# A new order of the ACT, DVE, POOL and SP queues in a fused attention, mixture and channel-mixing kernel on one Trainium2 core

## The chip, the cores and the metric

The kernel runs on one core of one Trainium2 chip. Its time is the device time of that core in microseconds. Three runs of the kernel before took 461.11, 462.46 and 463.20 us, so the median is 462.46 us. Every trace is one profiled execution. The engines are named as in the profile: PE is TensorE, PEld is its weight load, DVE is VectorE, ACT is ScalarE, POOL is GpSimd, and SP only issues DMAs here.

## The reference, cut to what matters

All data are float32. The batch is 2 and the sequence has 768 tokens.

```python
# A: attention with 8 heads of 64; a window of 96 keys behind the query and 8 global keys, a slope per head
scores = q @ k.T / 8 - slope[h] * dist          # masked outside window and global keys
x = softmax(scores) @ v                         # heads joined to 512 columns
# D: top 2 of 4 experts, each a causal attention with one head of 64
w = softmax over the two largest of x @ w_gate
x = sum over e in top2: w[e] * (softmax(causal((x @ wq[e]) @ (x @ wk[e]).T / 8)) @ (x @ wv[e]) @ wo[e])
# M: token mixing of rank 32, then a channel MLP
u = x + (x.T @ U @ V).T                         # U 768x32, V 32x768
out = u + relu(u @ w_ch1) @ w_ch2               # 512 -> 2048 -> 512
```

## The kernel before

The program is recorded as straight-line code, in three stages that overlap. In stage A there are twelve "pairs". A pair holds the scores of four blocks of 128 queries for two heads each, in two PSUM tiles `S`. Stage D has twelve more pairs (`d_pair`). For every pair PE computes scores (L475 or L423), DVE adds a mask and takes the row extreme (`least`, L427, eight instructions in stage A, output `nm`), ACT takes the exponentials (`soften`, L438, eight, input `nm`, row sums in `den`), DVE inverts the sums (L445 and L446, output `rec`), POOL scales the probabilities `pr` by `rec` (L451, eight), PE transposes them (L373, into the banks `T`, `U` and `acc`), ACT and DVE copy the transposes to SBUF (`moved`, tiles `pt`, L226 on ACT and L229 on DVE), and PE multiplies them with the values (L510 to L517 or L693, bank `X`). ACT then copies `X` to the high part of `xT` or to `zT` (L226), and DVE stores the low part (L232).

`position(r)` lays these steps out as a software pipeline: PE does the scores of pair r+1, then the values of pair r-1, then the transposes of pair r. From position 6 on PE also gets "fillers" between the transposes: the projections of stage D (`c_heads`, outputs `qk`, and `c_values`, outputs `v`, L554 and L555), and later the folded channel weights (`w_fold`, L766, outputs `wph` and `wpl`). They share the one bank `acc`. Every filler's result has to be copied out of that bank, by ACT or DVE (`qk`, `v`: L226 or L229), before PE can begin the next one. The pairs 0 to 6 have no filler among their first steps. The transition (L792 to L824) forms `zs` and `y`, and then stage M runs 64 steps of the MLP on PE.

Weights reach SBUF through four raw tiles `cr`, in a ring. The projection weights are split into a high part `wh` on POOL (L223) and a low part `wl` on DVE (L232, `wl<-cr,wh`, 772 columns, both inputs in SBUF). The float64 weights are narrowed by ACT (L240), POOL (L241) and DVE (L246, L247).

The code order sets only the dependencies and PE's own queue. `Body.in_order` (L1298) takes the recorded instructions, and the class `Order` gives each a cost (`length`, L90) and finds its predecessors (`before`, L118: data, buffer reuse, and PE in the recorded order). `Order.queues` (L166) returns one list for each engine, and `in_order` pins the list as that engine's instruction order. In the kernel before, `queues` is a greedy list scheduler: it goes forward in time, and at each moment that an engine is free it takes, of the instructions that are ready, the one with the longest remaining way to the end (`way`). It never looks back.

Of the kernel before, what the change touches and what calls it, by code (L numbers as in the profile page):

```python
# [1 line left out]

# [1 line left out]

# [57 lines left out]
class Order:  # L62
# [2 lines left out]

    SIGNAL, LAND, ISSUE, RATE = 70, 400, 1300, 300.0
    TURN = {
        ("row", "col"): 200, ("col", "T"): 152, ("T", "row"): 93, ("full", "row"): 150, ("col", "full"): 150,  # L70
        ("row", "T"): 200, ("full", "col"): 150, ("T", "col"): 150, ("row", "full"): 150}
# [92 lines left out]
            self.after[b].add(a)  # L164

    def queues(self):  # L166
        n = len(self.ins)
        succ = [[] for _ in range(n)]
        for k in range(n):
            for q in self.preds[k]:  # L170
                succ[q].append((k, self.eng[k] != self.eng[q] or self.bytes[q] > 0))
            for q in self.after[k] - self.preds[k]:
                succ[q].append((k, False))
        way = [0.0] * n
        for k in reversed(range(n)):
            land = self.lat[k] + self.SIGNAL
            if self.bytes[k]:
                land += self.ISSUE + self.LAND + self.bytes[k] / self.RATE
            way[k] = self.cost[k] + max([way[s] + (land if far else 0) for s, far in succ[k]], default=0)
        left, ready = [len(p | q) for p, q in zip(self.preds, self.after)], [0.0] * n  # L180
        open_, free, line, wire = {}, {}, {}, 0.0
        for k, e in enumerate(self.eng):
            open_.setdefault(e, set())
            free[e], line[e] = 0.0, []
            if not left[k]:
                open_[e].add(k)
        for _ in range(n):
            t, e = min((min(max(free[e], ready[k]) for k in s), e) for e, s in open_.items() if s)
            k = max((k for k in open_[e] if max(free[e], ready[k]) <= t), key=lambda k: (way[k], -k))
            open_[e].discard(k)  # L190
            line[e].append(k)
            end = free[e] = t + self.cost[k]
            done = end + self.lat[k]
            if self.bytes[k]:
                wire = max(end + self.ISSUE, wire) + self.bytes[k] / self.RATE
                done = wire + self.LAND
            for s, far in succ[k]:
                ready[s] = max(ready[s], done + self.SIGNAL if far else end)
                left[s] -= 1
                if not left[s]:  # L200
                    open_[self.eng[s]].add(s)
        return {e: [self.ins[k] for k in q] for e, q in line.items()}


class Pair:
# [1168 lines left out]
```

## Time and profile before

| quantity | value |
|---|---|
| median of three runs (lowest, highest) | 462.46 us (461.11, 463.20) |
| the profiled execution's own time | 461.54 us |
| its span, from the first to the last instruction | 459.7 us |
| PE busy | 435.0 us, 95% of the span |
| DVE, ACT, POOL busy | 236.6 us, 194.9 us, 118.2 us |
| mean granted TensorE clock | 0.99 |

The busy time of PE is modelled from the ends of pipelined matmuls, so it says that PE had something in flight, not that PE ran at its peak. The chain of work that ended last runs over PE for 62% of the span. Where a row ends in square brackets, the brackets give the idle time of the engine just before, and the engine, tile and line whose result ended it. The name of a tile is printed without its number in the trace. The order lists print it with its numbers.

### The profile page before, as it was taken

The page shows a single profiled execution, that of the slowest core. Times are in us where ns is not written, and L with a number is a line of the kernel's source. Part 1 is how long each engine was busy: PE and PEld are TensorE (multiplying, and loading weights), DVE is VectorE, ACT ScalarE, POOL GpSimd, SP SyncE. Part 2 cuts the span into 40 slices and gives each one's busy share as a digit, 9 for nine tenths or more (in the row PEclk, how much of TensorE's full clock was granted, in tenths as well). Part 3 has the DMA queues.
Part 4 walks back from the last instruction along what each step waited for, and adds up shares of the span by engine and source line. Part 5 has one row for each costly group of instructions (what it writes and reads, how often), then busy time and mean ns, then how long its engine had stood idle before and what let it go on. Part 6 is the DMA issues. An engine that isn't in the chain of part 4 may idle for free.

```text
span 459.7 us, 8926 instructions
## 1 busy us (share of the span) xinstructions
PE 435.0 (95%) x3388; PEld 370.1 (81%) x3388; DVE 236.6 (51%) x700; ACT 194.9 (42%) x541; POOL 118.2 (26%) x226
## 2 busy tenths in 40 slices
PE   4889999999999999999899999999999999999994
PEld 2567898889887877878688888888888888888883
DVE  4588665695746845876898996211121111211111
ACT  5778666566545434674654553211121111211111
POOL 7688823532324333345112230000000000000000
PEclk9799999999999999999999999999999999999999
DMA  7986706303413302344243430200001000200002
GB/s 279 315 268 196 243 8 177 72 2 134 148 43 93 92 1 91 93 140 138 91 138 98 143 126 4 68 0 1 0 9 61 1 0 0 70 0 1 0 1 76
DMA packets 17780, 39.35 MB, mean 86 GB/s; under 512 B 2688, under 2 KB 6528, under 8 KB 17728
## 3 DMA queue, kind: packets, MB, share of 16 engines
q1 hardware_dynamic: 15856, 37.11, 25.5%
q10 hardware_dynamic: 1872, 1.58, 1.0%
q8 instruction: 29, 0.48, 0.4%
q14 instruction: 23, 0.19, 0.1%
HBM read 35.53 MB, written 3.15 MB: 84 GB/s over the span
## 4 chain that ended last, share of the span: by engine, by line
PE 62%; issue 2%; DVE 1%; POOL 1%; ACT 1%; ACTq 0%; POOLq 0%; DVEq 0%
PE h L554 10%; PE acd L554 7%; PE acc L766 5%; PE h L555 5%; PE acc L554 5%; PE X L554 4%; PE acd L555 4%; PE T L554 4%; PE U L554 3%; PE X L693 2%; PE acc L555 2%; PE X L555 2%; PE T L555 2%; PE S L423 2%; PE U L555 2%
## 5 line engine op out<-in xcount | busy, mean ns | idle before, releaser
L848 DVE SCALAR_TENSOR_TENSOR pr<-h,pr 128x384 fp32r<-128x384 f32 x64 | 35.6, 556 | 134.8 <-ACT pr L847 134.6
L847 ACT ACTIVATE pr<-h 128x384 fp32r<-128x384 f32 x64 | 31.5, 492 | 150.5 <-PE h L555 150.5
L451 POOL TENSOR_SCALAR pr<-pr,rec 128x192 f32<-128x192 f32 (+5 forms) x144 | 73.7, 535 | 71.0 <-DVE rec L448 39.8
L438 ACT ACTIVATE pr<-pr,nm 128x192 f32<-128x192 f32 (+5 forms) x144 | 73.2, 511 | 42.3 <-DVE nm L427 42.2
L241 POOL TENSOR_SCALAR cr<-cr 128x512 f32<-128x512 f32 (+2 forms) x35 | 26.2, 750 | 85.4 <-ACT ct L240 62.8
L554 PE MATMUL acc<-xT,wh 128*128 128x384 f32 x128 | 34.4, 350 | 1.5 <-ACT qk L226 1.4
L427 DVE CUSTOM_DVE_ANT_0 pr<-S,cm 128x512 f32<-128x512 f32 (+3 forms) x48 | 24.7, 552 | 14.9 <-PE S L423 14.9
L766 PE MATMUL acc<-ct,woT 128*128 128x256 f32 x128 | 29.1, 380 | 0.4 <-DVE qk L229 0.4
L247 DVE SCALAR_TENSOR_TENSOR ct<-ct,cr 128x512 int32<-128x512 int32 (+2 forms) x35 | 28.2, 805 | 1.6
L475 PE MATMUL S<-kx,qr 64*64 64x192 f32 (+1 forms) x384 | 21.1, 359 | 6.7 <-ACT qr L398 6.3
L438 ACT ACTIVATION_READ_ACCUMULATOR pr<-pr,nm 128x1 f32 x144 | 27.2, 189 | 0.0
L246 DVE SCALAR_TENSOR_TENSOR cr<-cr 128x512 int32<-128x512 int32 (+2 forms) x35 | 24.5, 699 | 4.6 <-POOL cr L241 4.5
L240 ACT ACTIVATE ct<-cr 128x512 f32<-128x512 f32 (+2 forms) x35 | 22.8, 651 | 9.1 <-PE acc L766 8.5
L766 PEld LDWEIGHTS acc<-ct,woT 128*128 128x128 f32 x128 | 23.7, 190 | 3.6 <-DVE qk L229 0.7
L373 PE MATMUL T<-ident,pr 128*128 128x128 f32 x144 | 23.8, 280 | 1.5 <-POOL pr L451 0.8
L554 PE MATMUL acd<-w2h,pr 128*128 128x512 f32 x64 | 25.2, 394 | 0.0
L554 PE MATMUL acd<-w2l,pr 128*128 128x512 f32 x64 | 25.2, 394 | 0.0
L555 PE MATMUL acd<-w2h,pr 128*128 128x512 f32 x64 | 25.2, 394 | 0.0
L554 PEld LDWEIGHTS acc<-xT,wh 128*128 128x128 f32 x128 | 22.2, 188 | 3.6 <-ACT qk L226 2.6
L373 PE MATMUL U<-ident,pr 128*128 128x128 f32 x136 | 23.1, 281 | 1.9 <-POOL pr L451 1.8
L427 DVE CUSTOM_DVE_ANT_0 pr<-S,dw 128x192 f32<-128x192 f32 x80 | 23.5, 352 | 2.7 <-PE S L475 2.2
L475 PEld LDWEIGHTS S<-kx,qr 64*64 64x64 f32 x384 | 14.8, 150 | 10.9 <-ACT qr L398 6.6
(274 smaller groups left out, 1042.7 us busy)
## 6 DMA issues: line engine op xcount, KB each, us to landing
cr<-in_w_dram SPq DMA_DIRECT2D x32, 512.0 KB, 3.7
v<-in_vx_dram SPq DMA_DIRECT2D x8, 704.0 KB, 5.3
kx<-in_kx_dram SPq DMA_DIRECT2D x7, 464.0 KB, 5.8
qr<-in_q_dram SPq DMA_DIRECT2D x7, 384.0 KB, 4.4
vz<-in_vo_dram SPq DMA_DIRECT2D x16, 160.0 KB, 5.5
cr<-in_wall_dram SPq DMA_DIRECT2D x4, 386.0 KB, 6.1
out_dram<-o SPq DMA_DIRECT2D x12, 128.0 KB, 1.9
out_dram<-o ACTq DMA_DIRECT2D x12, 128.0 KB, 1.9
```

The source lines that it names most:

```text
L241: nc.gpsimd.tensor_scalar(hi.bitcast(F32), hi.bitcast(F32), 0.0, -0.0, op0=ALU.mult, op1=ALU.add)
L247: nc.vector.scalar_tensor_tensor(t, t, 3, lo, op0=ALU.logical_shift_left, op1=ALU.bitwise_or)
L373: self.nc.tensor.transpose(t[:, k * P : (k + 1) * P], s, self.ident)
L427: self.nc.vector.tensor_tensor_reduce(out=out, in0=sp, in1=mask, scale=scale, scalar=start, op0=ALU.add, op1=ALU.min, accum_out=nm)
L438: self.nc.scalar.activation(pr[:, h, :], pr[:, h, :], AF.Exp, bias=nm[h], scale=-1.0, accum_out=den[:, k, h : h + 1])
L451: nc.gpsimd.tensor_scalar(pr[:, h, :], pr[:, h, :], rec[:, k, h : h + 1], 0.0, op0=ALU.mult, op1=ALU.add)
L475: self.nc.tensor.matmul(sp[s][a * HB : (a + 1) * HB, h, o : o + w], q[hs, i * P + a * HB : i * P + (a + 1) * HB], k[hs, n : n + w], start= ...
L554: mm(out, lh, rh, start=first, stop=False), mm(out, lh, rl, start=False, stop=False),
L555: mm(out, ll, rh, start=False, stop=last)]
L766: nc.tensor.matmul(ac[:, p, :], self.woT[:, kc, p * P : (p + 1) * P], w1[kc // 2][:, kc % 2, :], start=kc == 0, stop=kc == 3)
L847: nc.scalar.activation(hh, hp, AF.Relu)
L848: nc.vector.scalar_tensor_tensor(hl, hp, 0.0, hh.bitcast(F32), op0=ALU.max, op1=ALU.subtract)
```

## The change

`Order.queues` is written anew. It still computes `way`, and it then lays all instructions out in time several times. A layout (`fit`) takes the instructions by rank, each as soon as its predecessors are placed, and puts each into the first gap on its engine that is long enough, also a gap that lies before instructions placed already. DMAs get a gap on a common "wire" as well. The first pass goes forward, ranked by `way`. Then a pass goes backward from the end (predecessors and successors exchanged), and the next forward pass is ranked by the ends that the backward pass gave. Three forward passes are made, and the one with the earliest modelled end gives the queues. The modelled wire rate goes from 300 to 350. The list of PE is the same in both kernels, instruction by instruction. The other four lists hold the same work in another order. The lines behind `queues` lie 26 lines later in the new kernel (L226 is L252 there, L438 is L464).

```diff
-from contextlib import ExitStack
+import bisect
+import heapq
...
@@ -65,7 +66,8 @@
 
 
 
-    SIGNAL, LAND, ISSUE, RATE = 70, 400, 1300, 300.0
+    TURNS = 3
+    SIGNAL, LAND, ISSUE, RATE = 70, 400, 1300, 350.0
     TURN = {
         ("row", "col"): 200, ("col", "T"): 152, ("T", "row"): 93, ("full", "row"): 150, ("col", "full"): 150,
         ("row", "T"): 200, ("full", "col"): 150, ("T", "col"): 150, ("row", "full"): 150}
@@ -164,42 +166,66 @@
             self.after[b].add(a)
 
     def queues(self):
+
+
         n = len(self.ins)
-        succ = [[] for _ in range(n)]
+        land = [self.lat[k] + self.SIGNAL + (self.ISSUE + self.LAND + self.bytes[k] / self.RATE if self.bytes[k] else 0) for k in range(n)]
+        fore = [[(q, land[q] if self.eng[k] != self.eng[q] or self.bytes[q] > 0 else 0) for q in self.preds[k]]
+                + [(q, 0) for q in self.after[k] - self.preds[k]] for k in range(n)]
+        back = [[] for _ in range(n)]
         for k in range(n):
-            for q in self.preds[k]:
-                succ[q].append((k, self.eng[k] != self.eng[q] or self.bytes[q] > 0))
-            for q in self.after[k] - self.preds[k]:
-                succ[q].append((k, False))
+            for q, d in fore[k]:
+                back[q].append((k, d))
         way = [0.0] * n
         for k in reversed(range(n)):
-            land = self.lat[k] + self.SIGNAL
-            if self.bytes[k]:
-                land += self.ISSUE + self.LAND + self.bytes[k] / self.RATE
-            way[k] = self.cost[k] + max([way[s] + (land if far else 0) for s, far in succ[k]], default=0)
-        left, ready = [len(p | q) for p, q in zip(self.preds, self.after)], [0.0] * n
-        open_, free, line, wire = {}, {}, {}, 0.0
-        for k, e in enumerate(self.eng):
-            open_.setdefault(e, set())
-            free[e], line[e] = 0.0, []
-            if not left[k]:
-                open_[e].add(k)
-        for _ in range(n):
-            t, e = min((min(max(free[e], ready[k]) for k in s), e) for e, s in open_.items() if s)
-            k = max((k for k in open_[e] if max(free[e], ready[k]) <= t), key=lambda k: (way[k], -k))
-            open_[e].discard(k)
-            line[e].append(k)
-            end = free[e] = t + self.cost[k]
-            done = end + self.lat[k]
-            if self.bytes[k]:
-                wire = max(end + self.ISSUE, wire) + self.bytes[k] / self.RATE
-                done = wire + self.LAND
-            for s, far in succ[k]:
-                ready[s] = max(ready[s], done + self.SIGNAL if far else end)
-                left[s] -= 1
-                if not left[s]:
-                    open_[self.eng[s]].add(s)
+            way[k] = self.cost[k] + max([way[s] + d for s, d in back[k]], default=0)
+        best = None
+        rank = [-w for w in way]
+        for turn in range(self.TURNS):
+            start = self.fit(rank, fore, back)
+            end = max(s + c for s, c in zip(start, self.cost))
+            if best is None or end < best[0]:
+                best = end, start
+            late = self.fit([-s - c for s, c in zip(start, self.cost)], back, fore, True)
+            rank = [-s - c for s, c in zip(late, self.cost)]
+        start = best[1]
+        line = {}
+        for k in sorted(range(n), key=lambda k: (start[k], k)):
+            line.setdefault(self.eng[k], []).append(k)
+        self.end = best[0]
         return {e: [self.ins[k] for k in q] for e, q in line.items()}
+
+    def fit(self, rank, fore, back, reverse=False):
+
+        n = len(rank)
+        left, ready, start = [len(f) for f in fore], [0.0] * n, [0.0] * n
+        heap = [(rank[k], k) for k in range(n) if not left[k]]
+        heapq.heapify(heap)
+        busy = {e: ([], []) for e in {*self.eng, "wire"}}
+
+        def place(e, s, c):
+            begins, ends = busy[e]
+            x = bisect.bisect_right(ends, s)
+            while x < len(begins) and begins[x] < s + c:
+                s = ends[x]
+                x += 1
+            begins.insert(x, s)
+            ends.insert(x, s + c)
+            return s
+
+        while heap:
+            _, k = heapq.heappop(heap)
+            c = self.cost[k]
+            s = start[k] = place(self.eng[k], ready[k], c)
+            late = 0
+            if self.bytes[k] and not reverse:
+                late = place("wire", s + c + self.ISSUE, self.bytes[k] / self.RATE) - s - c - self.ISSUE
+            for j, d in back[k]:
+                ready[j] = max(ready[j], s + c + d + (late if d else 0))
+                left[j] -= 1
+                if not left[j]:
+                    heapq.heappush(heap, (rank[j], j))
+        return start
 
 
 class Pair:
```

The first place is ACT in pair 3 of stage A, which has no filler. `pr_95` is that pair's probabilities and `nm_97` to `nm_105` are its eight row extremes. `xT_14<-X_94` are the copies of pair 1's output, and `pt_108` and `pt_111` are the copies of pair 2's transposes. Before:

```order
L438 ACTIVATE pr_95_489,den_96_490<-pr_95_489,nm_97_491 128x128
L438 ACTIVATE pr_95_489,den_96_490<-pr_95_489,nm_98_493 128x128
L438 ACTIVATE pr_95_489,den_96_490<-pr_95_489,nm_100_506 128x192
L438 ACTIVATE pr_95_489,den_96_490<-pr_95_489,nm_101_508 128x192
L226 ACTIVATE xT_14_94<-X_94_462 128x256
L438 ACTIVATE pr_95_489,den_96_490<-pr_95_489,nm_102_510 128x192
L226 ACTIVATE xT_14_94<-X_94_462 128x256
L226 ACTIVATE pt_108_535<-T_106_527 128x384
L438 ACTIVATE pr_95_489,den_96_490<-pr_95_489,nm_103_512 128x192
L438 ACTIVATE pr_95_489,den_96_490<-pr_95_489,nm_104_514 128x192
L438 ACTIVATE pr_95_489,den_96_490<-pr_95_489,nm_105_516 128x192
L226 ACTIVATE pt_111_547<-acc_110_543 128x384
```

Now:

```order
L464 ACTIVATE pr_95_489,den_96_490<-pr_95_489,nm_97_491 128x128
L252 ACTIVATE xT_14_94<-X_94_462 128x256 x2
L252 ACTIVATE pt_108_535<-T_106_527 128x384
L464 ACTIVATE pr_95_489,den_96_490<-pr_95_489,nm_100_506 128x192
L464 ACTIVATE pr_95_489,den_96_490<-pr_95_489,nm_101_508 128x192
L464 ACTIVATE pr_95_489,den_96_490<-pr_95_489,nm_102_510 128x192
L464 ACTIVATE pr_95_489,den_96_490<-pr_95_489,nm_103_512 128x192
L464 ACTIVATE pr_95_489,den_96_490<-pr_95_489,nm_104_514 128x192
L464 ACTIVATE pr_95_489,den_96_490<-pr_95_489,nm_105_516 128x192
L252 ACTIVATE pt_111_547<-acc_110_543 128x384
L464 ACTIVATE pr_95_489,den_96_490<-pr_95_489,nm_98_493 128x128
```

Four exponentials stood ahead of the first copy of `X_94`, and one does now. The exponential of `nm_98` went to the end, behind `pt_111`.

The second place is ACT beside the first `c_values` filler (`acc_255`, copied into `v_20`), with the exponentials of pair 8 (`pr_245`). Before:

```order
L438 ACTIVATE pr_245_1271,den_246_1272<-pr_245_1271,nm_249_1277 128x192
L438 ACTIVATE pr_245_1271,den_246_1272<-pr_245_1271,nm_250_1279 128x192
L226 ACTIVATE xT_16_96<-X_243_1233 128x256
L438 ACTIVATE pr_245_1271,den_246_1272<-pr_245_1271,nm_251_1281 128x192
L226 ACTIVATE xT_16_96<-X_243_1233 128x256
L438 ACTIVATE pr_245_1271,den_246_1272<-pr_245_1271,nm_252_1283 128x192
L438 ACTIVATE pr_245_1271,den_246_1272<-pr_245_1271,nm_253_1285 128x192
L438 ACTIVATE pr_245_1271,den_246_1272<-pr_245_1271,nm_254_1287 128x192
L226 ACTIVATE v_20_107<-acc_255_1301 128x260
L226 ACTIVATE pt_258_1323<-U_256_1314 128x384
L226 ACTIVATE pt_263_1350<-U_261_1342 128x384
```

Now:

```order
L464 ACTIVATE pr_245_1271,den_246_1272<-pr_245_1271,nm_249_1277 128x192
L252 ACTIVATE xT_16_96<-X_243_1233 128x256 x2
L464 ACTIVATE pr_245_1271,den_246_1272<-pr_245_1271,nm_250_1279 128x192
L464 ACTIVATE pr_245_1271,den_246_1272<-pr_245_1271,nm_251_1281 128x192
L252 ACTIVATE v_20_107<-acc_255_1301 128x260
L252 ACTIVATE pt_258_1323<-U_256_1314 128x384
L464 ACTIVATE pr_245_1271,den_246_1272<-pr_245_1271,nm_252_1283 128x192
L464 ACTIVATE pr_245_1271,den_246_1272<-pr_245_1271,nm_253_1285 128x192
L464 ACTIVATE pr_245_1271,den_246_1272<-pr_245_1271,nm_254_1287 128x192
L252 ACTIVATE pt_263_1350<-U_261_1342 128x384
L464 ACTIVATE pr_245_1271,den_246_1272<-pr_245_1271,nm_248_1275 128x128
```

The copy of the filler's bank stood behind six of these exponentials from `nm_249` on, and now stands behind three.

The third place is DVE around the reciprocal of pair 6 (`rec_193`), with the low parts `wl_104` of the projection weights. Before:

```order
L232 TENSOR_TENSOR xT_15_95<-X_167_818,xT_14_94 128x256
L232 TENSOR_TENSOR wl_104<-cr_117_565,wh_103 128x772
L232 TENSOR_TENSOR xT_15_95<-X_167_818,xT_14_94 128x256
L229 COPY pt_182_897<-U_180_887 128x384
L229 COPY pt_186_910<-T_185_905 128x384
L445 TENSOR_SCALAR rec_193_971<-den_169_846 128x8
L446 RECIPROCAL rec_193_971<-rec_193_971 128x8
L427 ISA pr_194_982,nm_196_984<-S_190_920,dw_148 128x192
```

Now:

```order
L258 TENSOR_TENSOR xT_15_95<-X_167_818,xT_14_94 128x256 x2
L255 COPY pt_182_897<-U_180_887 128x384
L255 COPY pt_186_910<-T_185_905 128x384
L258 TENSOR_TENSOR wl_104<-cr_68_331,wh_103 128x772
L471 TENSOR_SCALAR rec_193_971<-den_169_846 128x8
L472 RECIPROCAL rec_193_971<-rec_193_971 128x8
L258 TENSOR_TENSOR wl_104<-cr_91_442,wh_103 128x772
L258 TENSOR_TENSOR wl_104<-cr_117_565,wh_103 128x772
L258 TENSOR_TENSOR xT_15_95<-X_192_938,xT_14_94 128x512
L255 COPY pt_207_1019<-T_205_1013 128x384
L453 ISA pr_194_982,nm_196_984<-S_190_920,dw_148 128x192
```

Before, one `wl` stood here, well ahead of the reciprocal. Now three of the four stand around it, two of them directly behind it and ahead of pair 7's row extremes.

## Rows read from the trace of the kernel before

**Rows 1.** Stages in us: engine busy times, granted clock (PEclk), DMA share and rate.

```profile
13.00:20.30 7.30, 6.67 (x49) 4.03 (x51) 3.37 (x18) 4.68 (x21) 7.10 (x18) 0.55 1.05 321
20.30:50.80 30.50, 27.69 (x557) 22.45 (x553) 24.98 (x116) 24.69 (x100) 23.54 (x47) 1.00 0.77 241
...
229.50:452.40 222.90, 222.57 (x1065) 192.48 (x1066) 81.77 (x145) 56.12 (x113) 11.68 (x14) 1.00 0.12 38
```

**Rows 2.** What PE waited for: us in total, times, longest us.

```profile
PE U L373 <- POOL pr L451: 1.8, 1, 1.8
PE acc L554 <- ACT qk L226: 1.4, 3, 0.7
...
PE acc L554 <- ACT v L226: 1.1, 3, 0.5
PE S L821 <- DVE zs L232: 1.1, 1, 1.1
PE acc L373 <- ACT pt L226: 0.8, 1, 0.8
PE T L373 <- POOL pr L451: 0.8, 1, 0.8
PE T L373 <- ACT pt L226: 0.7, 2, 0.5
PE acc L554 <- DVE v L229: 0.5, 1, 0.5
```

**Rows 3.** Timeline of PE around the first values filler: start, length, what, wait.

```profile
69.75 0.28 PE L555 MATMUL acc<-wh,xT 128*128 128x260 f32 x1
...
71.15 0.39 PE L554 MATMUL acc<-wh,xT 128*128 128x260 f32 x1 [0.47 <-ACT v L226]
```

**Rows 4.** Timeline of ACT beside that filler.

```profile
70.73 0.37 ACT L226 ACTIVATE v<-acc 128x260 f32<-128x260 f32 x1
```

**Rows 5.** Timeline of DVE at the transition.

```profile
224.63 0.68 DVE L247 SCALAR_TENSOR_TENSOR ct<-ct,cr 128x512 int32<-128x512 int32 x1
225.45 0.41 DVE L232 TENSOR_TENSOR zs<-S,zs 32x256 fp32r<-32x256 f32 x1
```

**Rows 6.** Timeline of SP, the first loads.

```profile
0.74 0.87 SPq L390 DMA_DIRECT2D kx<-in_kx_dram  x2
1.66 1.37 SPq L389 DMA_DIRECT2D qr<-in_q_dram  x3
```

**Rows 7.** Timeline of ACT, stage A.

```profile
5.81 2.16 ACT L398 ACTIVATE qr<-qr 64x256 f32<-64x256 f32 x4 [3.35 <-DMA qr<-in_q_dram]
...
25.51 0.40 ACT L438 ACTIVATE pr<-pr,nm 128x128 f32<-128x128 f32 x1 [1.61 <-DVE nm L427]
...
26.74 0.44 ACT L438 ACTIVATE pr<-pr,nm 128x192 f32<-128x192 f32 x1
...
27.47 0.38 ACT L226 ACTIVATE xT<-X 128x256 fp32r<-128x256 f32 x1 [0.19 <-PE X L517]
```

**Rows 8.** Timeline of PE, stage A.

```profile
6.27 4.38 PE L475 MATMUL S<-kx,qr 64*64 64x128 f32 x48 [6.27 <-ACT qr L398]
...
13.63 0.82 PE L373 MATMUL U<-ident,pr 128*128 128x128 f32 x2 [1.78 <-POOL pr L451]
...
50.25 0.44 PE L373 MATMUL U<-ident,pr 128*128 128x128 f32 x2
...
50.78 0.42 PE L554 MATMUL acc<-xT,wh 128*128 128x384 f32 x1
```

**Rows 9.** POOL, line L451, in two stretches: ns minimum, median, maximum.

```profile
L451 POOL TENSOR_SCALAR pr<-pr,rec x8: 380/429/1132, 37.2 to 40.6; 128x192 f32<-128x192 f32 x6, 128x128 f32<-128x128 f32 x2
...
L451 POOL TENSOR_SCALAR pr<-pr,rec x8: 375/432/433, 49.0 to 51.7; 128x192 f32<-128x192 f32 x6, 128x128 f32<-128x128 f32 x2
```

**Rows 10.** Timeline of DVE, stage A.

```profile
39.34 1.00 DVE L232 TENSOR_TENSOR wl<-cr,wh 128x772 fp32r<-128x772 f32 x1
```

**Rows 11.** One microsecond, columns as in rows 1.

```profile
23.00:24.00 1.00, 0.22 (x2) 0.25 (x3) 0.98 (x3) 0.91 (x3) 0.61 (x2) 1.00 0.77 245
```

## The prediction

> **What bounds the kernel now.** I read the stage table first. From 229.50 to 452.40 us PE is busy 222.57 of 222.90 us [rows 1], and its own list is unchanged, so nothing can be won in stage M. DVE works 81.77 us there, and loses nothing in total by another order. What follows the last matmul, about 7 us, consists of copies and stores whose order is the same in both kernels. What an order of the other engines can change lies before 229.5 us, in what PE waits for, so I read PE's list of waits next [rows 2]. It has three kinds. The fillers wait for the copy that empties `acc`: three times an ACT `qk` (1.4 us in total), three times an ACT `v` (1.1) and once a DVE `v` (0.5), together 3.0 us. In the pairs without fillers PE waits for an ACT `pt` copy (0.8 and 0.7) or for POOL (1.8 and 0.8). At the transition it waits 1.1 for the DVE `zs`. Last I read the timelines of pairs 0 to 6, since between 20.30 and 50.80 us PE, DVE, ACT and POOL are busy 27.69, 24.98, 24.69 and 23.54 of 30.50 us [rows 1]. There four engines are nearly full, and a delay on one soon reaches PE.
>
> **Fillers.** The first `v` filler ends at 69.75 + 0.28, its copy starts only at 70.73 on ACT, and PE takes up the bank again at 71.15 after 0.47 us of waiting [rows 3, 4]. Between the two, ACT did exponentials. Now the copy stands ahead of three of them, at 0.44 us each [rows 7], so it starts nearly as soon as the filler ends, and PE's transposes cover it. The other two `v` copies, the `qk` copies and the DVE `v` copy move in the same way: on DVE the `v` copy now precedes the reciprocals. For one of the three `qk` copies the four exponentials still stand ahead, and it gains only if these start earlier, which they can, as two weight joins left the place ahead of their `least`. I take 2.9 of the 3.0 us, and at worst 2.0. The exponentials that fall behind are late for POOL by less than 1.5 us, and PE transposes that pair only after the next pair's scores and values, so I cost this at nothing. If that cover is gone, it is 0.44 for each exponential behind the copy.
>
> **Transition.** A DVE `ct` from 224.63 held `zs` until 225.45 [rows 5]. It has moved behind the `y` parts, and `zs` now waits for ACT alone. I take 0.3 of the 1.1 us; nothing and 1.1 are the bounds.
>
> **The pairs without fillers.** Four things change here.
> (a) The second load is now the first part of `qr`, which was third. SP issues one in about 0.44 us (0.87 for two) [rows 6], ACT waited for this load until 5.81, and PE started at 6.27 [rows 7, 8]. The issue alone gives 0.4, and no longer lying behind a `kx` load of 320 KB, at 321 GB/s [rows 1], up to 1.0 more. I take 0.6, because PE soon meets the exponentials, which do not go faster.
> (b) `pt` copies now precede exponentials, so the waits of 0.8 and 0.7 [rows 2] should go.
> (c) Against that, in pair 3 ACT did four exponentials between 25.51 and the first `xT` copy at 27.47, which waited for PE's `X` [rows 7]. Now it does one and then stands until `X` is done. Three, or 1.3 us, fall behind the copies. Pair 6 has the same new order (two fall behind, 0.9), and pair 2 has two behind `pt` and `xT` (0.9). An exponential late is a reciprocal late, POOL late, and a transpose late.
> (d) POOL. An L451 takes 0.43 us, but one in the first stretch took 1.132 [rows 9], and a `wl` of 1.00 us was on DVE then [rows 10]. So a `wl` beside L451 costs POOL 0.7. In the second stretch no `wl` ran, and the longest L451 was 0.433. The new order takes the `wl` away from pair 4 (0.7 won) and puts two directly behind `rec_193`, exactly where pair 6's L451 begin (1.4 lost).
>
> The Trainium skill (SBUF — State Buffer, section "SBUF: two separate sides") has a rule for this: a DVE instruction with two SBUF inputs and a GpSimd instruction that reads SBUF take turns on one port pair, held for a whole instruction, and the loser "fully blocks". The trace agrees (1.132 beside 0.43). Nothing in the new planner's costs knows of it. By the rule pair 6's place costs up to the two full `wl`, 2.0 us; by the row 1.4.
>
> Walked through pair by pair with these durations and PE's unchanged work, PE is ahead of before by 0.6 at pair 0's transposes, 0.7 at the end of pair 3's (the 1.3 of (c) eats what (b) gave), 1.4 at the end of pair 5's, and then loses 1.8 at pair 6: its L451 begin 1.0 earlier than the 49.0 of before [rows 9], the fourth is delayed by 1.4, and PE, which would arrive at its transposes 1.4 before 50.25, waits. The first filler, at 50.78 before [rows 8], then starts 0.4 later than before. So the term is +0.4. The lower bound is -1.4, the lead of pair 5 kept. The upper bound is +1.6: everything in (c) and (d) paid in full (1.3 + 0.9 + 0.9 + 1.4 - 0.7 = 3.8) less (a) and (b) (2.1), about.
>
> **Sum.** -2.9 - 0.3 + 0.4 = -2.8 us. The profiled execution's own time is 461.54, so 458.7. The median of the runs shown, 462.46, lies 0.9 above it, and the same difference applied there gives 459.7, which I predict. With the bounds of the terms, this case reaches from about 458.0 to 461.2.
>
> **Rivals.**
> 1. The lock does not bite. If the reciprocal of pair 6 comes so late that the two `wl` are not beside L451, or POOL gets the port first, the pairs without fillers keep the lead of 1.4. Sum -4.6, or 457.9. For it speaks that POOL needs only a little head start; against it, that the two `wl` stand directly behind the reciprocal that POOL waits for.
> 2. The gain is given back in the pairs without fillers. ACT executes its list in order, and a copy that waits for PE holds every exponential behind it [rows 7]. With the upper bound +1.6, and 2.0 instead of 2.9 for the fillers, the sum is -0.7, or 461.8, no change that can be told. For it speaks how full the four engines are there [rows 1]; against it, that waits of 1.5 us for `pt` are removed in the same place.
> 3. Slower: the clock. The granted clock was 0.50 of full in most of the stretch from 13 to 20.3 us, 0.55 on average [rows 1], so at the level of 1.2 GHz, after PE had stood 1.78 us [rows 8]. At pair 6 PE will stand 1 to 2 us between transposes, and at pair 3 about as long in pieces. A stretch like that one costs 7.3 x 0.45 = 3.3 us. Two of them give 459.7 + 6.6 = 466.3. It decides as soon as the granted clock falls once more after 20.3 us; one fall gives 463.0. Against it speaks that PE was busy only 0.22 us of the microsecond from 23 to 24 and the clock stayed at 1.00 [rows 11].
>
> **How the numbers follow.** I give the forecast 0.49, rival 1 0.17, rival 2 0.23 and rival 3 0.11. A measurement of this kernel tells about 0.5%, 2.3 us, from no change, so the limits are 460.1 and 464.8. The forecast's own range has some six tenths below 460.1: 0.30, with rival 1 0.17 and a little of rival 2 makes 0.49 for faster. Rival 2 and the rest of the forecast make 0.39 for the same, and rival 3 nearly alone 0.12 for slower. The range from 456.6 to 463.4 takes in rival 1 with its spread, rival 2, and a single fall of the clock.
>
> **What would show it.** In the new profile the waits of PE for ACT `qk` and ACT `v` should be nearly gone from the list, and the DVE `v` with them. PE's first matmul should start between 5.2 and 5.9 us. One or two L451 of pair 6 should take about 1.1 us with `wl` beside them, and the first filler should start near 51.2 us. From the first matmul of stage M to the last should again be 222.9 us. The forecast is wrong if new waits of the fillers appear, if stage M shows waits for `w2l`, or if the clock falls a second time.

## The result, and the profile after

The changed kernel takes 458.65 us (median of 5 runs, 457.33 to 459.10) beside 462.46 us (461.11 to 463.36) for the kernel before in the same comparison. The ratio is 0.9899, with a 95% interval from 0.9872 to 0.9926, so it is faster by 0.7 to 1.3%. Forecast were 459.7 us and a change of -2.8; measured is -3.8. The profiled execution is the slowest of the five: 459.10 us with a span of 457.3, beside 461.54 and 459.7 before. It shows only 2.4 us of the gain, and why is the first thing to explain.

What PE waited for (us in total, times, longest), the answer to [rows 2]:

```profile
PE S L501 <- ACT qr L424: 5.0, 1, 5.0
PE U L399 <- POOL pr L477: 3.1, 4, 1.5
PE h L580 <- ACT y01h L252: 1.2, 1, 1.2
PE S L847 <- DVE zs L258: 1.1, 1, 1.1
PE acc L792 <- DVE qk L255: 0.6, 1, 0.6
PE acc L580 <- DVE qk L255: 0.4, 1, 0.4
```

The fillers' waits for ACT `qk`, ACT `v` and DVE `v` are gone. Two waits for DVE `qk`, which the prediction's list left out, remain (0.43 and 0.43 before, 0.43 and 0.57 now). PE starts at 5.0 instead of 6.3. The `zs` wait stands as it was. For POOL PE waits 3.1 us in all where it was 2.9 (1.8, 0.8 and 0.3). Two stretches that answer to [rows 1], with stage M now from 225.4 on (engine busy times, granted clock, DMA share and rate):

```profile
20.30:50.80 30.50, 27.88 (x528) 21.41 (x524) 23.55 (x100) 23.36 (x93) 24.20 (x48) 1.00 0.80 262
225.40:450.40 225.00, 224.68 (x1066) 193.71 (x1066) 81.94 (x147) 56.54 (x114) 10.51 (x14) 0.99 0.13 40
```

Stage M, whose order nobody changed for PE, has grown from 222.9 to 224.6 us between its first and last matmul. Single microseconds of the same view at its start show why:

```profile
226.00:227.00 1.00, 0.86 (x5) 0.87 (x6) 1.00 (x3) 0.00 (x0) 0.00 (x0) 0.96 0.00 0
227.00:228.00 1.00, 1.00 (x4) 0.90 (x3) 0.91 (x3) 0.81 (x2) 0.00 (x0) 0.50 0.00 0
...
229.00:230.00 1.00, 1.00 (x4) 0.80 (x3) 1.00 (x3) 0.00 (x0) 0.52 (x1) 0.50 0.80 320
230.00:231.00 1.00, 1.00 (x6) 0.77 (x4) 0.90 (x3) 0.63 (x1) 0.00 (x0) 0.83 0.11 16
```

The granted clock was 0.50, the level of 1.2 GHz, for some 3.4 us, after PE had stood idle 1.07, 1.20 and 0.29 us in the transition:

```profile
221.83 0.61 PE L847 MATMUL S<-vs,zs 96*128 96x384 f32 x2 [1.07 <-DVE zs L258]
...
225.43 0.41 PE L580 MATMUL h<-y00h,wph 128*128 128x384 f32 x1 [1.20 <-ACT y01h L252]
226.13 0.44 PE L580 MATMUL h<-y00l,wph 128*128 128x384 f32 x1 [0.29 <-DVE y00l L258]
```

That cost 1.6 us: in the table below, M is 224.5 to 224.6 in the six profiles with such a fall in M, and 223.4 or less in the others.

Where PE stands at three places gives the account. The table has the start of the first filler (first `acc` of `xT` and `wh`), of the first matmul of stage M, and of the last matmul, from each run's PE timeline. Each row is one profiled execution, and the runs behind the first two rows are told in the next section:

| run | first filler | first M | last | fillers to M | M |
|---|---|---|---|---|---|
| before | 50.78 | 229.54 | 452.48 | 178.76 | 222.9 |
| changed | 51.29 | 225.43 | 450.00 | 174.14 | 224.6 |
| again | 51.48 | 225.63 | 448.58 | 174.15 | 223.0 |
| old_then_new | 52.42 | 226.57 | 451.12 | 174.15 | 224.6 |
| new_then_old | 51.63 | 230.72 | 455.24 | 179.09 | 224.5 |
| copies_only | 52.40 | 228.20 | 451.18 | 175.80 | 223.0 |
| swap_only | 50.82 | 229.58 | 452.59 | 178.76 | 223.0 |
| old_swap_new | 50.87 | 225.02 | 449.64 | 174.15 | 224.6 |
| rate300 | 53.49 | 227.63 | 450.99 | 174.14 | 223.4 |
| turns1 | 51.44 | 225.53 | 450.10 | 174.09 | 224.6 |
| wl_moved | 51.20 | 225.37 | 449.90 | 174.17 | 224.5 |
| warm | 52.42 | 230.22 | 452.60 | 177.80 | 222.4 |
| warm2 | 52.73 | 226.85 | 449.81 | 174.12 | 223.0 |
| best | 50.17 | 224.28 | 447.27 | 174.11 | 223.0 |

From the first filler to stage M the new lists need 174.1 to 174.2 us in every execution but warm, whose added matmuls wait, the old ones 178.8 (179.1 in new_then_old): a gain of 4.6. Before the first filler the changed kernel is 0.5 behind the profile of before, and the clock takes 1.6 in M. -4.6 + 0.5 + 1.6 = -2.5 at the last matmul, which is what the two profiles differ by.

How a copy that starts earlier pays is seen at the first values filler. PE, start and length (compare [rows 3]):

```profile
70.10 0.28 PE L581 MATMUL acc<-wh,xT 128*128 128x260 f32 x1
70.22 0.49 PE L399 MATMUL U<-ident,pr 128*128 128x128 f32 x3
70.55 0.49 PE L399 MATMUL T<-ident,pr 128*128 128x128 f32 x3
70.86 0.39 PE L580 MATMUL acc<-wh,xT 128*128 128x260 f32 x1
```

The same place in the kernel before:

```profile
70.20 0.49 PE L373 MATMUL T<-ident,pr 128*128 128x128 f32 x3
71.15 0.39 PE L554 MATMUL acc<-wh,xT 128*128 128x260 f32 x1 [0.47 <-ACT v L226]
```

From the start of the last transposes to the start of the filler it is 0.31 us now and was 0.95, so 0.64 were won where the list said 0.47. Now the filler starts before the transposes have ended (70.86 lies inside 70.55 + 0.49). Before, it started 0.47 after their end (70.20 + 0.49). The overlap of 0.18 is no part of the listed wait. ACT (compare [rows 4]) starts the copy 0.04 after the filler ends instead of 0.70:

```profile
70.42 0.39 ACT L252 ACTIVATE v<-acc 128x260 f32<-128x260 f32 x1
```

### The profile page after: what moved, and what is told of

Same layout as the page of the kernel before. It is cut to its first block, busy times and chain, and to the rows that moved or that the text cites. A ratio compares the mean times of both kernels' runs of the same rounds, so it can differ in the third digit from the quotient of the medians.

```text
span 457.3 us, 8918 instructions
## 1 busy us (share of the span) xinstructions
PE 437.1 (96%) x3388; PEld 371.2 (81%) x3388; DVE 238.2 (52%) x700; ACT 196.7 (43%) x541; POOL 118.5 (26%) x226
## 3 DMA queue, kind: packets, MB, share of 16 engines
HBM read 35.53 MB, written 3.15 MB: 85 GB/s over the span
## 4 chain that ended last, share of the span: by engine, by line
PE 88%; DVE 3%; ACT 3%; POOL 3%; issue 1%; DMA 1%; ACTq 0%; SPq 0%; POOLq 0%; DVEq 0%
PE acc L580 11%; PE h L580 10%; PE acd L580 7%; PE acc L792 6%; PE acc L581 5%; PE h L581 5%; PE S L449 4%; PE X L719 4%; PE X L580 4%; PE S L501 4%; PE acd L581 4%; PE T L580 4%; PE U L580 3%; PE T L399 3%; PE U L399 3%; POOL pr L477 3%
## 5 line engine op out<-in xcount | busy, mean ns | idle before, releaser
L477 POOL TENSOR_SCALAR pr<-pr,rec 128x192 f32<-128x192 f32 (+5 forms) x144 | 75.6, 546 | 98.8 <-DVE rec L474 52.4
L464 ACT ACTIVATE pr<-pr,nm 128x192 f32<-128x192 f32 (+5 forms) x144 | 73.3, 514 | 29.8 <-DVE nm L453 28.9
L267 POOL TENSOR_SCALAR cr<-cr 128x512 f32<-128x512 f32 (+2 forms) x35 | 24.9, 714 | 54.1 <-ACT ct L266 29.8
L464 ACT ACTIVATION_READ_ACCUMULATOR pr<-pr,nm 128x1 f32 x144 | 27.5, 191 | 0.0
L501 PE MATMUL S<-kx,qr 64*64 64x192 f32 (+1 forms) x384 | 22.2, 364 | 5.2 <-ACT qr L424 5.0
L255 DVE COPY pt<-T 128x384 f32<-128x384 f32 (+1 forms) x26 | 15.8, 609 | 14.6 <-PE T L399 14.3
```

The source lines that it names most:

```text
L267: nc.gpsimd.tensor_scalar(hi.bitcast(F32), hi.bitcast(F32), 0.0, -0.0, op0=ALU.mult, op1=ALU.add)
L464: self.nc.scalar.activation(pr[:, h, :], pr[:, h, :], AF.Exp, bias=nm[h], scale=-1.0, accum_out=den[:, k, h : h + 1])
L477: nc.gpsimd.tensor_scalar(pr[:, h, :], pr[:, h, :], rec[:, k, h : h + 1], 0.0, op0=ALU.mult, op1=ALU.add)
L501: self.nc.tensor.matmul(sp[s][a * HB : (a + 1) * HB, h, o : o + w], q[hs, i * P + a * HB : i * P + (a + 1) * HB], k[hs, n : n + w], start= ...
```

## The experiments

**The same kernel again**, with a blank line added:

```diff
     TURNS = 3
+
     SIGNAL, LAND, ISSUE, RATE = 70, 400, 1300, 350.0
```

> The changed kernel once more, with a blank line added. Theory A (the clock's second fall belongs to this execution, not to the order): the 0.50 stretch does not start at 226.9 us again, and the place of the falls differs from the first profile while first matmul (5.0 us), first filler (51.3) and first matmul of stage M (225.4) stay within 0.2 us. Theory B (the fall is caused by the new order at the transition): the granted clock falls again at 226.9, for about 3.4 us. Time 457.3 to 459.1 in both.

458.22 us, ratio 0.9887 (0.9858 to 0.9917). The granted clock was 0.50 from 12.8 to 19.7 us, in one piece, and stayed at 1.00 through the transition:

```profile
225.60:449.00 223.40, 223.04 (x1066) 192.53 (x1066) 81.91 (x147) 56.44 (x114) 10.54 (x14) 1.00 0.12 41
```

In the first profile of the changed kernel it was low from 15.3 to 18.7, and then again from 226.9 to 230.3. So theory A holds: the places of the falls belong to the execution, and the lists don't fix them. With 3.4 us more of low clock before 20 us the first filler came only 0.2 later (51.48 beside 51.29).

**Where the gain lies: old lists first, new behind**, and the reverse. `listed` is the old planner, and the lists are joined at the planned start of the first filler:

```diff
-        start = best[1]
-        line = {}
-        for k in sorted(range(n), key=lambda k: (start[k], k)):
+        first, rest = self.listed(), best[1]
+        cut = next((first[k] for k, e in enumerate(self.eng) if e == "PE" and self.aps(self.ins[k].ins)[0].dtype != F32), 0.0)
+        start, line = best[1], {}
+        for k in sorted(range(n), key=lambda k: (0, first[k], k) if first[k] < cut else (1, rest[k], k)):
```

> Old lists up to the planned start of the first filler, new lists behind it. Theory A (the whole gain lies in the fillers, 4.6 us, and the new order of the pairs without fillers loses 0.5): first filler at 50.8, waits for ACT qk, ACT v and DVE v gone, first matmul of stage M at 224.9 to 225.1, time 457.5 to 458.3, that is 0.3 to 1.0 faster than the changed kernel on the same chip. Rival (the earlier loads and pt copies are worth something behind the first filler): stage M starts later than 225.6 and the time is not below the changed kernel's.

459.02 us, ratio 0.9894 (0.9861 to 0.9927).

The reverse is the same with the two planners exchanged:

> New lists up to the planned start of the first filler, old lists behind it. Theory A: first filler at 51.3, the seven waits of the fillers back (3.0 us in the list of waits), first matmul of stage M at 229.7 to 230.2, time 462.3 to 463.5, no gain over the kernel before. Rival (part of the gain comes from the pairs without fillers): below 461.5.

464.19 us, ratio 1.0019 (0.9998 to 1.0041). The new lists in the fillers bring the gain of the fillers, 174.15 instead of 178.76, and the old ones bring it back to 179.09, with the seven waits and a fourth one for ACT `qk`. The time lies above the 462.3 to 463.5 expected. But old_then_new was not faster than the changed kernel, as theory A had it, and the signs of its rival came true (stage M at 226.57): its first filler began at 52.42 and not at 50.78, with the very lists of before. PE waited twice for `qr` there:

```profile
6.50 1.78 PE L540 MATMUL S<-kx,qr 64*64 64x128 f32 x16 [6.50 <-ACT qr L463]
8.43 3.48 PE L540 MATMUL S<-kx,qr 64*64 64x192 f32 x32 [0.15 <-ACT qr L463]
```

Also, new_then_old shows a fall of the clock in M (231.4 to 234.8) with the old lists in the transition, which goes some way to explain its time.

**Only the copies**: the kernel before, with six copies moved up in ACT's list.

```diff
+        q = line["Activation"]
...
+        for s, up in (("acc_255_", 2), ("acc_281_", 2), ("acc_307_", 1), ("acc_331_", 2), ("acc_487_", 2), ("acc_516_", 2)):
...
+                    q.insert(x - up, q.pop(x))
```

> The kernel before with six moves on ACT and nothing else: each of the six copies that PE's fillers waited for goes one or two instructions forward, ahead of exponentials (and of ct or cmp). Theory A (the gain of the fillers is the place of these copies): the waits of acc for ACT qk and ACT v leave the list; each is worth its listed wait and 0.18 more, the overlap of two matmuls that the wait takes away, so that from the first filler to stage M it is 175.2 to 175.8 us instead of 178.76 (3.4 of the 4.6 us that the changed kernel gains there), time 3.0 to 3.5 below the kernel before. Theory B (a listed wait is worth just what it says): 2.5 less, 176.3. Rival C (the rest of the new order is needed for it, since the exponentials moved behind the copies come too late): less than 1.5.

459.80 us, ratio 0.9924 (0.9907 to 0.9941), and 175.80 us from the first filler to M: 2.96 won. The six waits were listed with 2.56, of which 0.3 (one ACT `v`) still stands beside the DVE `v`:

```profile
PE acc L561 <- DVE v L236: 0.6, 1, 0.6
...
PE acc L561 <- ACT v L233: 0.3, 1, 0.3
```

So 2.3 of listed wait gave 3.0. Rival C falls, and theory B too; theory A's 175.8 is just reached. Six places in one list carry two thirds of what the whole new order gains in the fillers. This run, too, has the old order of loads, and its first filler began at 52.40.

**Only the loads**: the kernel before, with SP's second and third load exchanged.

```diff
+        q = line["SP"]
+        if len(q) < 1000 and n < 5000:
+            q[1], q[2] = q[2], q[1]
```

> The kernel before with one change: SP issues the first part of qr second instead of third. In two runs with the old order of loads the second qr part made PE wait again and the first filler began at 52.4, not at 50.8 as in the first profile of before. Theory A (that is the usual execution, and the load's place is worth over 1 us): first matmul at 4.9 to 5.2, no second wait for qr over 0.3, first filler 50.8 to 51.4, first filler to stage M 178.7 to 178.9, time 1.0 to 1.6 below the kernel before. Rival (PE only meets the exponentials earlier): first matmul earlier, but first filler at 52 or later, time within 0.5 of before.

462.01 us, ratio 0.9965 (0.9948 to 0.9982), 1.2 us below the 463.17 of the kernel before; the first filler at 50.82. So theory A holds by the times, and the load's place is worth 1.5 us at the first filler beside old_then_new and copies_only (52.4 to 50.8). The profiled execution of before had the first filler at 50.78 with the old loads. Of the three profiles with the old loads and the old pairs it was the early one, and beside it the load gains nothing. That the late start is the usual one rests on the other two profiles and on the times.

**The same loads for both orders of the pairs**: old_then_new with this exchange.

> As old_then_new (old lists up to the first filler, new behind it), with the first part of qr second on SP. It sets the old order of the pairs without fillers beside the new one with the same first loads. Theory A (the new order of these pairs wins with pt copies about what it loses with the wl beside L477): first filler 50.8 to 51.6 as in the changed kernel, ratio to before 0.986 to 0.990. Rival B (the lock of wl makes the new order worse there): first filler before 50.6, time over 0.7 below the changed kernel's. Rival C (the new order is better): first filler 51.8 or later.

458.73 us, ratio 0.9884 (0.9856 to 0.9912), the first filler at 50.87 where the new lists put it at 51.2 to 51.6. In the profiles the old order of the pairs without fillers is better by 0.3 to 0.8, inside theory A's range; the times don't tell the two apart.

**The planner's two constants.** `RATE` 350 to 300, and `TURNS` 3 to 1:

> The changed kernel with the planner's DMA rate at 300 as before instead of 350. Theory A (the rate only shifts planned starts in the pairs without fillers): first filler to stage M 174.0 to 174.3, first filler 50.5 to 52, time within 1.0 of the changed kernel. Rival (the rate is part of the gain): over 1.5 slower.

> The changed kernel with one forward pass instead of passes to and fro (TURNS 1). Theory A (placing each instruction in the first gap by rank does the work, the passes back add little): first filler to stage M 174 to 175.2, time within 1.5 of the changed kernel. Rival (the passes back are what moves copies ahead of exponentials): waits of the fillers return, 177 to 179 there, time 461.5 to 463.

With 300, 461.11 us, ratio 0.9962 (0.9948 to 0.9977). The fillers keep their 174.14, but SP's list begins `kx`, `kx`, `qr` again, PE's first matmul starts at 6.51, and the first filler at 53.49. The rival was right: this one number puts the small load second. The first filler is 2 us earlier by it, but not by the load alone, since 300 also moves other instructions (a `wl` on DVE from 31 to 51 us, small POOL work at the start, and a `ct` ahead of `y01h` on ACT; stage M took 0.4 more). With one forward pass 459.49 us, ratio 0.9929 (0.9909 to 0.9949): every stage in the profile is within 0.15 of the changed kernel's (first filler 51.44 beside 51.29), so placing by rank into gaps does the work, and the passes back add nothing that can be told. That its runs lie about 1 us above those of the changed kernel, in another comparison, stays unexplained.

**The lock of `wl`.** In the changed kernel the two `wl` behind `rec_193` stand beside POOL's L477, as predicted. DVE and POOL (compare [rows 9, 10]):

```profile
47.93 1.80 DVE L258 TENSOR_TENSOR wl<-cr,wh 128x772 fp32r<-128x772 f32 x2
```

```profile
48.18 4.47 POOL L477 TENSOR_SCALAR pr<-pr,rec 128x128 f32<-128x128 f32 x8 [1.93 <-DVE rec L472]
```

The eight L477 take 4.47 us where they took 3.14, and PE meets it in front of the first filler:

```profile
49.94 0.68 PE L399 MATMUL U<-ident,pr 128*128 128x128 f32 x2 [0.71 <-POOL pr L477]
50.70 0.84 PE L399 MATMUL T<-ident,pr 128*128 128x128 f32 x3
51.29 0.59 PE L580 MATMUL acc<-xT,wh 128*128 128x384 f32 x2
```

The experiment moves three of the four `wl` to places in front of `pt_139`, `pt_160` and `rec_193`:

```diff
...
+        for k, s in zip(joins, ("pt_139_", "pt_160_", "rec_193_")):
+            b = at(s)
+            if b is not None:
+                q.remove(k)
+                q.insert(q.index(b), k)
```

> The changed kernel with three of the four wl moved on DVE to places without a normal of POOL beside them. Theory A (DVE's wl holds POOL's L477 off): in pair 3 no L477 of 1.0 us and PE's waits for POOL of 0.16 and 0.76 at 31.5 to 32.6 gone; in pair 6 one wl beside L477 instead of two, the eight L477 last 3.6 to 3.9 instead of 4.47 us; first filler at 50.0 to 50.7 instead of 51.3; time 0.6 to 1.3 below the changed kernel. Rival (DVE's own time counts, not the lock): the pt copy and the reciprocal behind the moved wl come 0.95 later, first filler at 51.3 or later, time the same or up to 1 us longer.

458.09 us, ratio 0.9884 (0.9855 to 0.9912), no different from the changed kernel. POOL:

```profile
31.00 3.12 POOL L488 TENSOR_SCALAR pr<-pr,rec 128x128 f32<-128x128 f32 x8 [1.10 <-DVE rec L483]
...
36.76 3.83 POOL L488 TENSOR_SCALAR pr<-pr,rec 128x192 f32<-128x192 f32 x8 [1.76 <-DVE rec L483]
...
48.89 3.66 POOL L488 TENSOR_SCALAR pr<-pr,rec 128x128 f32<-128x128 f32 x8 [2.13 <-DVE rec L483]
```

The lock did what theory A says of POOL: pair 3's stretch fell from 3.88 to 3.12, pair 6's from 4.47 to 3.66. But a moved `wl` locked pair 4's (3.83 instead of 3.15), and the reciprocals behind them came later, so that pair 6's L488 began at 48.89 instead of 48.18. Another moved `wl` was itself held: it began behind a POOL `qr` of 0.91 us at 34.10, and took 1.63 us instead of 0.95.

```profile
34.18 1.63 DVE L269 TENSOR_TENSOR wl<-cr,wh 128x772 fp32r<-128x772 f32 x1
```

The first filler came at 51.20, within 0.1 of the changed kernel's. Both theories held for a part of the way, and took each other's effect away.

**PE busy in the transition.** Idle matmuls where PE waits, first into unused columns of `S` (7 and 8 of them), then into `acc` (4 and 5):

```diff
+        idle = self.bank("acc")[:, :P]
+        self.spin(idle, 4)
...
+        self.spin(idle, 5)
```

> The changed kernel with 7 and 8 idle matmuls (a transpose by the identity into unused columns) added on PE where it waits for zs and for y01h at the transition. Theory A (the fall of the granted clock at the start of stage M, 1.6 us, follows PE's idle microseconds there): granted clock 1.00 at the start of stage M, first to last matmul of M 222.9 to 223.0 in the profiled run, median 0.5 to 1.5 below the changed kernel's and a narrower spread. Theory B (the fall comes at its own time, whatever PE does there): it stands in this profile too or the median is the same. Rival C (the added matmuls come in the way of zs or y): stage M starts over 0.3 later behind the first filler than 174.15, time up to 1 us longer.

461.33 us, ratio 0.9956 (0.9937 to 0.9974). Rival C, with more than its 1 us: the added matmuls (two instructions each in the trace) waited themselves, as the trace has it for DVE `zs`, which reads other columns of the same bank, and came behind the wait instead of in it:

```profile
222.94 1.83 PE L840 MATMUL S<-ident 128*128 128x128 f32 x14 [1.07 <-DVE zs L258]
```

> As warm, but with 4 and 5 idle matmuls, into the bank acc, which nobody reads then, so that they wait for nobody. Theory A (the fall of the granted clock at the start of stage M follows PE's idle microseconds there): granted clock 1.00 from 215 to 250 us, first to last matmul of M 222.9 to 223.0, first filler to stage M 174.1 to 174.4, median 0.4 to 1.2 below the changed kernel's (ratio to before 0.985 to 0.988). Theory B (it comes at its own time): a 0.50 stretch near 227 us or a ratio as the changed kernel's, 0.988 to 0.990.

458.30 us, ratio 0.9880 (0.9856 to 0.9904). Now they fill the waits for `zs` and `y01h`, and M takes 223.0. But the clock fell at another place, between the transposes of pairs 3 and 4, from 35.2 to 38.6 us:

```profile
34.00:35.00 1.00, 0.90 (x5) 0.51 (x5) 0.91 (x2) 1.00 (x7) 1.00 (x3) 1.00 0.94 363
36.00:38.00 2.00, 2.00 (x30) 1.16 (x22) 1.25 (x8) 0.67 (x3) 1.66 (x5) 0.50 0.16 49
```

There too PE had stood before, 0.15 and 0.75 us for POOL in pair 3. In the changed kernel's profile it stood 0.16 and 0.76 there, and the clock stayed at 1.00. The scores that PE does between these transposes, here and in the changed kernel's profile:

```profile
35.20 2.84 PE L501 MATMUL S<-kx,qr 64*64 64x192 f32 x32
```

```profile
35.35 1.53 PE L501 MATMUL S<-kx,qr 64*64 64x192 f32 x32
```

The lists up to 217 us are those of the changed kernel, so the order does not set this fall. Whether the added instructions have a part in it (warm and warm2 have it, `best` below has not) is open. The first filler came at 52.73, over 1.2 late, and what M won was lost. (In warm the clock fell at nearly the same place, 34.8 to 38.2, and its first filler came at 52.42.) So the profile shows theory A's signs in the transition and in M, and the time shows theory B's: 458.30 is not below the changed kernel's. The run does not decide between them.

**Together**: old_swap_new with the idle matmuls of warm2. Up to 217 us its lists are those of old_swap_new.

> old_swap_new (old lists up to the first filler with the first part of qr second, new lists behind it) with the 4 and 5 idle matmuls of warm2 in the transition. Theory A (the terms add: first filler 50.9, first filler to stage M 174.1, no fall of the clock at stage M): last matmul at 447.8 to 448.2, time 456.3 to 457.5, ratio to before 0.983 to 0.987. Theory B (the fall of the clock comes anyway, or its price is paid elsewhere): a 0.50 stretch near 226 us or a median of 458 or more.

456.45 us (455.95 to 457.91), ratio 0.9864 (0.9836 to 0.9891), the fastest of all. First filler 50.17, and stage M:

```profile
224.30:447.70 223.40, 223.04 (x1066) 192.46 (x1066) 81.83 (x147) 56.46 (x114) 10.44 (x14) 1.00 0.12 41
```

Its interval overlaps with that of old_swap_new, so the gain of the idle matmuls is not told apart by times. Its first filler at 50.17 beside 50.87 shows how far two executions of one order lie apart. Of the eleven profiles without idle matmuls six show the fall in M (224.5 to 224.6 us), of the three with them none, but two of these three have one ahead of pair 4's transposes instead. That the idle matmuls save a fall is not shown.

## Why the prediction was right, and where it was not

- **Fillers, -2.9.** The mechanism is shown (old_then_new, new_then_old, copies_only), the size was too small: with the transition, which gave nothing, 4.6. Lined up instruction by instruction, PE's lead grows by 0.64, 0.46, 0.41, 0.37, 0.78, 0.61 and 0.92 at the seven places, 4.2 in all, where the waits listed there (0.47, 0.43, 0.23, 0.40, 0.52, 0.37 and 0.66) make 3.1; the rest are shifts below 0.2. The term was mis-sized at "2.9 of the 3.0 us": a listed wait begins at the end of the last matmul, and now the next starts before that end. At five of the seven places that gave 0.17 to 0.26 beyond the listed wait, at the other two nothing; why these differ stays open. The `qk` copy that still stands behind all its exponentials did gain, by earlier exponentials (0.61). The term "at nothing" for the exponentials behind the copies held: from the first filler to stage M no new wait stands in PE's list.
- **Transition, -0.3.** This step failed. Nothing came: the wait was 1.08 and is 1.07. I had named the DVE `ct` that ended at 225.31. ACT, in the kernel before, was as late:

```profile
225.92 0.62 PE L821 MATMUL S<-vs,zs 96*128 96x384 f32 x2 [1.08 <-DVE zs L232]
```

```profile
224.66 0.76 ACT L226 ACTIVATE zs<-S 32x256 fp32r<-32x256 f32 x2 [1.49 <-PE S L555]
```

It ends at 225.42, and the DVE `zs` began at 225.45 [rows 5]. Now DVE stands free from 220.41 and still begins only behind ACT's `zs`:

```profile
221.37 0.41 DVE L258 TENSOR_TENSOR zs<-S,zs 32x256 fp32r<-32x256 f32 x1 [0.95 <-ACT zs L252]
```

- **Pairs without fillers, +0.4.** Against the profiled execution 0.5 came out, the first filler at 51.29 where 51.2 was forecast. The way there was nearly as walked through: PE was 0.29 ahead at pair 0's first transposes (0.6 forecast), 0.70 at the last ones of pair 3 (0.7) and 1.30 at the last ones of pair 5 (1.4), and lost 1.81 at pair 6 (1.8). The waits for ACT `pt` of 0.8 and 0.7 went, and pair 6's POOL stretch grew by 1.33 where 1.4 was forecast, though as one L477 of 1.71 us, the first, and not as one or two of 1.1. The Trainium skill (SBUF — State Buffer, section "SBUF: two separate sides") is borne out: the first L477 beside the two `wl` ended only when they did. But part (a), the load, at 0.6, was mis-sized. Beside this profile of before it gains nothing (swap_only, 50.82), and beside the other two profiles with the old loads and pairs 1.5 (52.4 to 50.8). Against 52.4 the whole term is about -1.0. The base was not the usual one, as far as these profiles and the times tell, and this is the likely reason why the medians gained more than the profiles: I carried the 0.9 between profile and median over to the new kernel, but much of it seems to have lain in the start that the change mended.
- **Stage M, 0.** Its 222.9 became 224.6 in the profiled execution, by a mechanism that I had as rival 3, at a place I had not named and at half the price: 1.6 for one fall, not 3.3. Ahead of pair 4's transposes a fall cost 1.3 (warm2, 2.84 beside 1.53), and before 20 us two executions with 3.4 us of low clock more or less lie 0.2 apart at the first filler. A second fall of the clock was named as a sign that the forecast is wrong. It came, and the time was in the range all the same, since the fall cost half and the fillers gave 1.7 more than forecast. The fall does not need the change: it is there with the old lists (new_then_old) and not there in another execution of the changed kernel (again). Whether the new lists make it more frequent is not shown: without idle matmuls five of seven profiles with the new lists in the transition have it, and one of four with the old ones.
- **The other rivals.** Rival 1 fails, as the lock bit, though its 457.9 lies nearer to the measured 458.65 than the forecast does. Rival 2 fails: the pairs give back 0.5 in the profiles, not the gain.
- **First matmul** at 4.99, a little before the 5.2 to 5.9 expected.

With the late start as base the account reads: fillers -4.6, load -1.5 (-1.2 by the times of swap_only), new order of the pairs +0.5, about -5.6, less what the clock takes in some executions. Measured were -3.8 and, in the comparison of again, -4.95. No run splits the difference. The range held the time; the median of 458.65 lies 1.0 below the forecast, as two misses of the same sign (fillers, load) met two of the other (transition, clock). That the number came so near is in part luck.

## What to carry to other kernels

Read what a wait costs from start to start of the instructions around it, against the same pair where there is no wait: here that gave about 0.2 more than the list for five of seven waits. Before a profile's times become the base of a forecast, see whether its execution was a usual one: where it lies below the median, ask which stage was lucky, and whether the change touches that stage. And when a planner moves hundreds of instructions, look for the few that PE waits for: six copies (3.0 us) and the order of two loads (1.2 to 1.5 us) make up most of this change.

## What the runs showed of the hardware that was not expected

- The granted clock fell to 0.50 for some 3.4 us at the start of stage M in six of eleven executions without idle matmuls, after the idle microseconds of the transition, and cost 1.5 to 1.6 us each time; in two with idle matmuls it fell ahead of pair 4's transposes. All fourteen profiles have a first low stretch between 12 and 23 us, of 3.4 us (eight) or 6.8 (six). Where it falls differs between executions of one kernel.
- Two `wl` on DVE, one right behind the other, held the first of POOL's L477 until both were done, though that L477 had begun before the second of them: 1.33 us in all (4.47 beside 3.14). The other way round, a `wl` that began behind a POOL `qr` took 1.63 us instead of 0.95 (wl_moved).
- The first DMA loads differ between executions with one and the same list: the first matmul came at 6.27 or at 6.50 to 6.56, but the first filler at 50.8 or at 52.4. In the late ones PE waited for the second part of `qr` as well (0.15 us in old_then_new, 0.54 in copies_only).
